# Routed attention and a gelu layer: ten sums of the first batch go to VectorE, and three batches make their first layer's combinations in PSUM

## Chip, core and metric

The kernel runs on one core of a Trainium2 chip. Its time is the device time of one execution in microseconds (us). TensorE (PE in the profile) multiplies matrices and writes to PSUM, VectorE (DVE), ScalarE (ACT) and GpSimd (POOL) work on tiles, and SyncE (SP) issues the transfers. GpSimd takes no part in PSUM work in this kernel.

## The reference, cut to what matters

```python
# q, k, v: (4 batches, 8 heads, 768, 64); centroids: (8, 16, 64)
q_assign = argmax(normalised(q) @ normalised(centroids).T)
k_assign = argmax(normalised(k) @ normalised(centroids).T)
scores = where(q_assign == k_assign, q @ k.T / 8, -1e9)
attn   = softmax(scores) @ v                       # per head
x = attn, heads side by side                       # (3072, 512)
h = x @ w_in                                       # (3072, 2048)
g = h / (1 + exp(-1.702 * h))                      # gelu, quick form
out = g @ w_out                                    # (3072, 512), float32
```

## The kernel before, in words

**Order.** Instructions are written out by hand in the order in which each engine runs them; engines wait for one another through semaphores. First comes attention for all four batches (0 to about 342 us). Its result stays in SBUF for batch 1 and is kept in DRAM (`kept`) for the others. Then come, for each batch `b` of 0 to 3, a first layer (`w_in`) and a second layer (`w_out`). This text counts batches from 1, so `b == 0` is batch 1.

**First layer.** Both layers use a block method that makes seven products of half-size blocks in place of eight (Strassen's method in the form of Winograd). For each of the eight blocks `f`, `first7` (line 848) makes seven products of two 128x384 matmuls (`product`, L854), each into a PSUM bank of its own out of the six of `ps_b`. Operands are blocks of `w_in`, sums of such blocks (`W`, made two blocks ahead on GpSimd by `sums_w`), tiles `x`, and sums of those (`Tx2`, `Tx3`, `Tx4`, also called T2 to T4; `x_steps` makes them for the next batch on VectorE during `k` = 5 and 6 of the second layer). The seven products are combined to four results, `G[:, f]` and `G[:, f + 8]` with two halves each: one ScalarE copy (L864) and seven VectorE adds with one operand in PSUM (`add`, L845), then four gelus in place (`finish`, L859). `after7(f - 1)` then makes one difference of `G` and, from `f` = 5 on, slices of the sums that the second layer needs first (`Y`, `E`).

**Second layer.** `second49(k, ...)` runs for `k` = 0 to 6, in the order `ORDER = (1, 2, 3, 6, 5, 7, 4)` of the outer products `i`. Each makes seven products of four 128x192 matmuls (L904). Three of its banks, called x, z and v, are used: after x has been copied out by ScalarE, further products are added onto what stands in it (`start=False`). The weights are blocks of `w_out`, sums of those (`Z`), and for three of the seven products sums of sums, `Wz` (three of 128x512 per `k`), which are made in batch 1 by `keep_w` on GpSimd, kept in DRAM as `kept_w`, and loaded again for each later batch by `load_sums`. For `k` = 5 and 6 of batch 1, `load_sums(k, made=True)` makes them in the tile that is used at once. During `k`, VectorE makes the four sums t3, t2, t1, t4 for `k + 1` (`sums_t`), in the steps of `extra`. At the end of `k`, the result `y` is added to the output sums `Y`:

```python
pool = nc.vector if last and i in (5, 7) else nc.gpsimd
sums(pool, {1: (),
            2: ((Y[11], y, "+", Y[22]),),
            3: ((Y[12], y, "+", Y[22]),),
            6: ((Y[12], y, "+", Y[12]), (Y[21], y, "+", Y[22])),
            5: ((Y[12], y, "+", Y[12]), (Y[22], y, "+", Y[21])),
            7: ((Y[22], y, "+", Y[22]), (Y[21], y, "+", Y[21]))}[i])
```

`last` is true in the last batch only. All elementwise sums outside PSUM go through `sums` and so have one line, L598, on whichever engine runs them; they are told apart by tile and shape. The SP queue carries all loads and stores, in the order of the program.

Of the kernel before, what the change touches and what calls it, by code (L numbers as in the profile page):

```python
# [8 lines left out]
FP32 = mybir.dt.float32  # L9
# [4 lines left out]
AF = mybir.ActivationFunctionType  # L14
# [24 lines left out]
def fast(  # L39
# [26 lines left out]
    nc = tc.nc  # L66

    B, H, S, D = q.shape
    NC = centroids.shape[1]
    DM, DF = moe_w_in.shape  # L70
    P = 128
    NJ = S // P
    HALF = S // 2
# [14 lines left out]
    FB = NF // 2  # L88
# [507 lines left out]
    def sums(engine, todo):  # L596
        for o, a, op, b in todo:
            engine.tensor_tensor(out=o, in0=a, in1=b, op=(  # L598
                ALU.add if op == "+" else ALU.subtract))
# [3 lines left out]
    def A_in(row, col, f):  # L603

        at = (row * FB + f) * P
        return w_in[:, 2 * col:2 * col + 2, at:at + P]

    w_of = {}
# [162 lines left out]
        a = W_of(i)  # L771
        sums(nc.vector, ((a(0, 1), a(0, 0), "-", a(0, 1)),))

    def keep_w(k, o):

        a = W_of(ORDER[k])
        s2, s1, s4 = o
        for i, (o, x, op, z) in enumerate((
                (s2, a(1, 1), "-", a(0, 1)), (s1, s2, "+", a(0, 0)),
                (s4, a(1, 0), "-", s2))):  # L780
            sums(nc.gpsimd, ((o, x, op, z),))
            nc.sync.dma_start(out=kept_w[k, i], in_=o)

    def spare_y():
# [5 lines left out]
    def load_sums(k, made=False):  # L790
        W[k] = ws.tile([P, 3, FQ, P], FP32, name="Wz")
        if made:
            keep_w(k, [W[k][:, i] for i in range(3)])
            return
        for i in range(3):
            nc.sync.dma_start(out=W[k][:, i], in_=kept_w[k, i])
# [47 lines left out]
    def add(o, p, a):  # L844
        nc.vector.tensor_tensor(out=o, in0=p, in1=a, op=ALU.add)  # L845

    def first7(b, f, X, T):

        S = w_of.pop(b * FB + f)

        def product(a, x):
            ps = ps_b.tile([P, 512], FP32, name="b")
            for c in range(2):
                nc.tensor.matmul(out=ps[:, 0:HALF], lhsT=a[:, c], rhs=x(c),  # L854
                                 start=(c == 0), stop=(c == 1))
            return ps[:, 0:HALF]

        def finish(g):
            nc.scalar.activation(out=g, in_=g, func=AF.Gelu_apprx_sigmoid,  # L859
                                 scale=2.0)  # L860

        g1, g2 = G[:, f], G[:, f + FB]
        p = product(A_in(0, 0, f), lambda c: X[0, 0, c])
        nc.scalar.copy(g1[:, 0], p)  # L864
        p = product(S[2], lambda c: T[2, c])
        add(g2[:, 1], p, g1[:, 0])
        p = product(S[1], lambda c: T[1, c])
        add(g1[:, 1], p, g2[:, 1])
        p = product(S[3], lambda c: T[3, c])
        add(g2[:, 0], p, g2[:, 1])  # L870
        add(g2[:, 1], p, g1[:, 1])
        p = product(S[4], lambda c: X[1, 1, c])
        add(g1[:, 1], p, g1[:, 1])
        finish(g2[:, 1])
        p = product(A_in(1, 1, f), lambda c: T[4, c])
        add(g2[:, 0], p, g2[:, 0])
        finish(g1[:, 1])
        p = product(A_in(0, 1, f), lambda c: X[1, 0, c])
        add(g1[:, 0], p, g1[:, 0])
        finish(g2[:, 0])  # L880
        finish(g1[:, 0])

    def after7(f):

# [5 lines left out]
    def second49(k, extra, last):  # L890

        i = ORDER[k]
        a, g, t, w = W_of(i), G_of(i), temps(k), W.pop(k)
        A = {1: a(0, 0), 2: a(1, 0), 3: w[:, 2], 4: a(1, 1), 5: w[:, 1],
             6: w[:, 0], 7: a(0, 1)}
        M = {1: g(0, 0), 2: g(1, 0), 3: g(1, 1), 4: t[4], 5: t[1], 6: t[2],
             7: t[3]}

        def bank_b():
            return ps_b.tile([P, 512], FP32, name="b")[:, 0:QT]  # L900

        def product(ps, n, start):
            for f in range(FQ):
                nc.tensor.matmul(out=ps, lhsT=A[n][:, f], rhs=M[n][:, f],  # L904
                                 start=start and f == 0,
                                 stop=(f == FQ - 1), skip_group_check=True)

        y = Y[22] if i == 1 else ep.tile([P, 2, HALF], FP32, name="y")
        y11, y12, y21, y22 = (y[:, m, q * QT:(q + 1) * QT]
                              for m in range(2) for q in range(2))  # L910
        p5 = ep.tile([P, QT], FP32, name="p5")
        x = bank_b()
        product(x, 1, True)
        nc.scalar.copy(y11, x)
        z = bank_b()
        product(z, 2, True)
        add(y11, z, y11)
        extra(0)
        product(x, 6, False)
        nc.scalar.copy(y12, x)  # L920
        v = bank_b()
        product(v, 5, True)
        nc.scalar.copy(p5, v)
        product(x, 7, False)
        nc.scalar.copy(y22, x)
        add(y22, y22, p5)
        extra(1)
        product(v, 3, False)
        add(y12, v, y12)
        if i == 4:  # L930
            c = Y[21]
            add(c[:, 0], y[:, 0], c[:, 0])
            add(c[:, 1, QT:], y22, c[:, 1, QT:])
            extra(2)
        product(x, 4, False)
        if i == 4:
            add(c[:, 1, 0:QT], x, c[:, 1, 0:QT])
            return
        nc.scalar.copy(y21, x)
        extra(2)  # L940
# [7 lines that stand above are left out]
# [79 lines left out]
    pend = iter(())  # L1027
    for b in range(B):
        for f in range(FB):
            first7(b, f, *XT)  # L1030
            sums_w(b * FB + f + 2)
            if f:
                after7(f - 1)
            do(pend, 1)
            if b == 0 and f < 3:
                for n in range(3 * f, min(3 * f + 3, FB)):
                    sums_z((nc.gpsimd, nc.vector, nc.vector)[n % 3], n)
            if b == 0 and f in (3, 4):
                for i in ORDER[0:4] if f == 3 else ORDER[4:]:
                    turn_w(i)  # L1040
            if b == 0 and f >= 3:
                for k in {3: (0,), 4: (1, 2), 5: (3,), 6: (4,), 7: ()}[f]:
                    keep_w(k, spare_y())
                if 5 <= f < 7:
                    load_sums(f - 5)
        after7(FB - 1)
        if b < B - 1:
            for h in range(2):
                for hp in range(HP):
                    x = xT_of[b + 1, h, hp] = xp.tile([P, HALF], FP32,  # L1050
                                                      name="x")
                    nc.sync.dma_start(out=x, in_=kept[b, h, hp])
            made = sums_x(b + 1)
        else:
            made = iter(())

        def stores(b, *todo, **how):
            for n in todo:
                store(b, n, **how)
                yield  # L1060

        def tail():
            store(b, 22)
            yield

        def chain(*todo):
            for steps in todo:
                yield from steps

        def sums_of_x():  # L1070
            for XT[:] in made:
                yield

        x_steps = sums_of_x()
        final = b == B - 1

        for k in range(7):
            nxt = sums_t(k + 1) if k < 6 else iter(())
            more = {1: sums_G(6), 2: sums_G(5), 3: sums_G(4),
                    4: stores(b, 11), 5: stores(b, 12) if final else x_steps,  # L1080
                    6: tail() if final else x_steps}.get(k, iter(()))
            if b == B - 1 and k < 2:
                test(k)
            if (b, k) == (B - 1, 6):
                is_bad = nc.values_load(bad[0:1, 0:1], min_val=0, max_val=1)

            def extra(at):
                do(nxt, (2, 1, 1)[at])
                do(more, ((1, 0, 1) if final else (0, 4, 4))[at] if k == 6
                   else (0, 0, 4)[at] if k == 2 else (0, 2, 2)[at])  # L1090

            second49(k, extra, final)
            if k < 5:
                load_sums(k + 2, b == 0 and k > 2)
            elif b < B - 1:
                load_sums(k - 5)
        pend = () if final else stores(b, 12, 22, 21)
        if final:
            store_last(b)
# [439 lines left out]
```

## Time and profile before

| what | value |
|---|---|
| median of 3 runs | 901.17 us (900.03 to 901.57) |
| profiled execution | 900.34 us |
| its span, first to last instruction | 898.5 us |
| PE, DVE, ACT, POOL busy | 885.8, 728.3, 366.1, 497.4 us |
| mean granted clock of TensorE | 0.999 |
| L845 adds on `G` (one operand in PSUM) | 224, mean 556 ns |
| L864 copies of `G` out of PSUM | 32, mean 478 ns |
| L859 gelus | 128, mean 523 ns |
| L598 POOL `Y` sums, 128x768 | 28, mean 2421 ns |

A line of a group or of an order of time names line, engine, operation, what is written and read, shape and number; a bracket gives the idle time before it and what ended it. Matmuls and weight loads are listed apart (PE, PEld), and each float32 matmul appears as two records, so a product of two matmuls has four records. Ends of matmuls are modelled; starts are the better guide. The layers of the four batches lie at about 342 to 414 and 414 to 481, 481 to 555 and 555 to 619, 619 to 691 and 691 to 755, 755 to 827 and 827 to 892 us.

### The profile page before, as it was taken

To read this page: it belongs to the slowest core of one execution; us is meant where nothing else is said; L and a number is where in the kernel's file an instruction comes from. 1 tells how busy PE (TensorE), PEld (TensorE's weight loads), DVE (VectorE), ACT (ScalarE), POOL (GpSimd) and SP (SyncE) were. 2 spreads that over 40 slices of the span, in tenths; PEclk is the share of its full clock that TensorE was granted. 3 is DMA by queue.
4 is the path that set the end of the run, shared out by engine and by line. 5 is a ranking of instruction groups with operands and counts; after the bars stand their busy time and mean duration, and the time that the engine had idled before them with its cause. 6 is when DMAs were issued, how large, how long until landed. Compare 5 with 4: busy or idle time off the path is not lost.

```text
span 898.5 us, 17781 instructions
## 1 busy us (share of the span) xinstructions
PE 885.8 (99%) x6720; PEld 581.4 (65%) x6720; DVE 728.3 (81%) x1183; ACT 366.1 (41%) x819; POOL 497.4 (55%) x469
## 2 busy tenths in 40 slices
PE   8999999999999999999999999999999999999997
PEld 3444444444444445558996557998556998556996
DVE  4999989999999997998998556798556798556795
ACT  3677767777677764322111232111232111222111
POOL 5899999998999998693274221143121134120130
PEclk9999999999999999999999999999999999999999
DMA  9566556666575310036113202223202223200224
GB/s 175 122 129 112 103 120 130 143 143 133 133 139 119 85 43 19 0 122 230 71 54 107 52 1 71 84 74 107 53 1 70 73 76 117 43 10 0 71 71 109
DMA packets 176333, 78.97 MB, mean 88 GB/s; under 512 B 152824, under 2 KB 159472, under 8 KB 176240
## 3 DMA queue, kind: packets, MB, share of 16 engines
q1 hardware_dynamic: 175984, 77.63, 35.2%
q8 instruction: 55, 0.90, 0.4%
q14 instruction: 38, 0.31, 0.1%
q10 hardware_dynamic: 256, 0.13, 0.1%
HBM read 61.03 MB, written 16.70 MB: 87 GB/s over the span
## 4 chain that ended last, share of the span: by engine, by line
PE 87%; DVE 8%; issue 2%; POOL 1%; DMA 1%; ACT 0%; SPq 0%; DVEq 0%; ACTq 0%; POOLq 0%
PE b L854 32%; PE b L904 23%; PE s L472 13%; PE o L537 12%; PE s L495 3%; PE m L554 3%; DVE G L598 2%; DVE E L598 2%; POOL sum L521 1%; PE m L348 1%; DVE Tx L598 1%; DMA in<-in_k_dram 1%; DVE x L598 0%; DVE e L200 0%; DVE y L845 0%
## 5 line engine op out<-in xcount | busy, mean ns | idle before, releaser
L521 POOL TENSOR_TENSOR sum<-sum,A 128x384 f32<-128x384 f32 x252 | 265.5, 1091 | 25.7 <-ACT A L503 16.6
L845 DVE TENSOR_TENSOR G<-b,G 128x384 f32<-128x384 f32 x224 | 123.1, 556 | 98.7 <-PE b L854 89.5
L503 ACT ACTIVATE A<-s 128x768 f32<-128x768 f32 x192 | 146.3, 809 | 91.1 <-PE s L495 71.0
L598 POOL TENSOR_TENSOR Y<-y,Y 128x768 f32<-128x768 f32 x28 | 67.4, 2421 | 175.0 <-DVE y L845 151.0
L859 ACT ACTIVATE G<-G 128x384 f32<-128x384 f32 x128 | 66.3, 523 | 199.1 <-DVE G L845 197.7
L472 PE MATMUL s<-T,T 64*64 64x384 f32 x1536 | 142.9, 487 | 0.7 <-ACT A L503 0.7
L537 PE MATMUL o<-A,inv 64*64 64x384 f32 x1536 | 141.2, 483 | 0.0
L598 POOL TENSOR_TENSOR W<-w_in 128x256 f32<-128x256 f32 x32 | 23.6, 737 | 163.8 <-PE b L854 163.5
L598 DVE TENSOR_TENSOR G<-G 128x768 f32<-128x768 f32 (+1 forms) x92 | 104.5, 1159 | 0.0
L472 PEld LDWEIGHTS s<-T,T 64*64 64x64 f32 x1536 | 54.9, 132 | 70.1 <-ACT A L503 36.4
L854 PE MATMUL b<-x,W 128*128 128x384 f32 x256 | 93.1, 486 | 0.0
L854 PE MATMUL b<-Tx,w_in 128*128 128x384 f32 x256 | 93.1, 486 | 0.0
L854 PE MATMUL b<-x,w_in 128*128 128x384 f32 x256 | 88.6, 486 | 0.0
L537 PEld LDWEIGHTS o<-A,inv 64*64 64x64 f32 x1536 | 58.3, 133 | 38.5 <-issue 33.5
L854 PEld LDWEIGHTS b<-x,W 128*128 128x128 f32 x256 | 48.6, 190 | 33.9
L854 PEld LDWEIGHTS b<-Tx,w_in 128*128 128x128 f32 x256 | 48.6, 190 | 33.9
L854 PEld LDWEIGHTS b<-x,w_in 128*128 128x128 f32 x256 | 48.5, 190 | 33.5 <-issue 0.6
L904 PE MATMUL b<-G,w_out 128*128 128x192 f32 x320 | 55.9, 326 | 0.0
L904 PEld LDWEIGHTS b<-G,w_out 128*128 128x128 f32 x320 | 52.7, 190 | 1.1
L904 PE MATMUL b<-E,Wz 128*128 128x192 f32 x288 | 51.5, 328 | 1.4 <-DVE E L598 1.4
L904 PEld LDWEIGHTS b<-E,Wz 128*128 128x128 f32 x288 | 47.1, 190 | 3.4 <-POOL Wz L598 1.3
L854 PE MATMUL b<-Tx,W 128*128 128x384 f32 x128 | 46.6, 487 | 1.5 <-DVE Tx L598 1.5
(169 smaller groups left out, 1366.4 us busy)
## 6 DMA issues: line engine op xcount, KB each, us to landing
Wz<-kept_w SPq DMA_DIRECT2D x78, 256.0 KB
raw<-in_moe_w_in_dram SPq DMA_DIRECT2D x16, 512.0 KB
raw<-in_moe_w_out_dram SPq DMA_DIRECT2D x16, 512.0 KB
inv<-in_v_dram SPq DMA_DIRECT2D x16, 384.0 KB
in<-in_q_dram SPq DMA_DIRECT2D x60, 96.0 KB
in<-in_k_dram SPq DMA_DIRECT2D x60, 96.0 KB
kept<-x SPq DMA_DIRECT2D x24, 192.0 KB
x<-kept SPq DMA_DIRECT2D x24, 192.0 KB
```

The source lines that it names most:

```text
L348: nc.tensor.matmul(out=ps[r:r + SQ, w * NJ * SQ:(w + 1) * NJ * SQ] .rearrange("p (j t) -> p j t", t=SQ), lhsT=cT[:, p % HP].rearrange("p a ...
L472: nc.tensor.matmul(out=ps[c:c + D, a, 0:HALF], lhsT=T[p, 1][rows, kt * P + c:kt * P + c + D], rhs=T[p, 0][rows, h * HALF:(h + 1) * HALF], ...
L495: nc.tensor.matmul(out=s_of[u][c:c + D, a, :], lhsT=rows_of[1, p % 2][rows, kt * P + c:kt * P + c + D], rhs=rows_of[0, p % 2][rows, h * HA ...
L503: nc.scalar.activation(out=A_of[u], in_=s_of.pop(u), func=AF.Exp, scale=SCALE)
L521: nc.gpsimd.tensor_tensor(out=sum_of[g][:, a], in0=(A_of[u - 1] if kt == 1 else sum_of[g])[:, a], in1=A_of[u][:, a], op=ALU.add)
L537: nc.tensor.matmul(out=o_of[g][a * D:(a + 1) * D, r, 0:HALF], lhsT=v_in[p][rows, a, kt, :], rhs=A[rows, a, :], start=(kt == 0), stop=(kt = ...
L554: nc.tensor.matmul(out=ps[a * D:(a + 1) * D, 0:HALF], lhsT=twos, rhs=sm[:, a, :], start=(i == 0), stop=(i == len(parts) - 1))
L598: engine.tensor_tensor(out=o, in0=a, in1=b, op=(ALU.add if op == "+" else ALU.subtract))
L845: nc.vector.tensor_tensor(out=o, in0=p, in1=a, op=ALU.add)
L854: nc.tensor.matmul(out=ps[:, 0:HALF], lhsT=a[:, c], rhs=x(c), start=(c == 0), stop=(c == 1))
L859: nc.scalar.activation(out=g, in_=g, func=AF.Gelu_apprx_sigmoid, scale=2.0)
L904: nc.tensor.matmul(out=ps, lhsT=A[n][:, f], rhs=M[n][:, f], start=start and f == 0, stop=(f == FQ - 1), skip_group_check=True)
```

## The change

Three edits. In `load_sums`, the sums `Wz` that batch 1 makes for its own `k` = 5 and 6 are made by VectorE instead of GpSimd (six instructions). In batch 1, as in the last batch already, VectorE instead of GpSimd adds `y` to the output sums for `i` = 5 and 7 (four instructions). And batches 2 to 4 use a new `first7_psum`: the same seven products, in another order, into three banks x, z and v, where x takes four products one upon another and v two; the results are read between them. It has three ScalarE copies and three VectorE adds in place of one and seven, and one of the four gelus reads PSUM. Batch 1 keeps `first7`.

```diff
-    def keep_w(k, o):
+    def keep_w(k, o, engine=nc.gpsimd):
...
-            sums(nc.gpsimd, ((o, x, op, z),))
+            sums(engine, ((o, x, op, z),))
             nc.sync.dma_start(out=kept_w[k, i], in_=o)
...
         if made:
-            keep_w(k, [W[k][:, i] for i in range(3)])
+            keep_w(k, [W[k][:, i] for i in range(3)], nc.vector)
             return
...
+    def first7_psum(b, f, X, T):
+
+        S = w_of.pop(b * FB + f)
+
+        def product(ps, a, x, start=True):
+            for c in range(2):
+                nc.tensor.matmul(out=ps, lhsT=a[:, c], rhs=x(c),
+                                 start=start and c == 0, stop=(c == 1),
+                                 skip_group_check=True)
+
+        def bank_b():
+            return ps_b.tile([P, 512], FP32, name="b")[:, 0:HALF]
+
+        def finish(g, ps=None):
+            nc.scalar.activation(out=g, in_=g if ps is None else ps,
+                                 func=AF.Gelu_apprx_sigmoid, scale=2.0)
+
+        g1, g2 = G[:, f], G[:, f + FB]
+        x, z, v = (bank_b() for _ in range(3))
+        product(x, A_in(0, 0, f), lambda c: X[0, 0, c])
+        nc.scalar.copy(g1[:, 0], x)
+        product(z, A_in(0, 1, f), lambda c: X[1, 0, c])
+        add(g1[:, 0], z, g1[:, 0])
+        product(x, S[2], lambda c: T[2, c], False)
+        nc.scalar.copy(g1[:, 1], x)
+        finish(g1[:, 0])
+        product(v, S[1], lambda c: T[1, c])
+        nc.scalar.copy(g2[:, 1], v)
+        product(x, S[3], lambda c: T[3, c], False)
+        add(g2[:, 1], x, g2[:, 1])
+        finish(g2[:, 1])
+        product(v, S[4], lambda c: X[1, 1, c], False)
+        add(g1[:, 1], v, g1[:, 1])
+        finish(g1[:, 1])
+        product(x, A_in(1, 1, f), lambda c: T[4, c], False)
+        finish(g2[:, 0], x)
...
-            first7(b, f, *XT)
+            (first7_psum if b else first7)(b, f, *XT)
...
-            second49(k, extra, final)
+            second49(k, extra, b in (0, B - 1))
```

## The prediction, made before the result

> **What bounds the kernel now.** I first read the page's busy shares and its chain of waits, then the stage table (busy time per stretch), then the order of time on each engine in the stages that the change touches.
>
> ```profile
> PE 885.8 (99%) x6720; PEld 581.4 (65%) x6720; DVE 728.3 (81%) x1183; ACT 366.1 (41%) x819; POOL 497.4 (55%) x469
> PE 87%; DVE 8%; issue 2%; POOL 1%; DMA 1%; ACT 0%; SPq 0%; DVEq 0%; ACTq 0%; POOLq 0%
> ```
>
> TensorE (PE) is busy 99%; VectorE (DVE) holds 8% of the chain. The stage table (stretch, length, busy time of PE, weight loads, DVE, ACT and POOL with their records, granted clock, DMA) says where: batch 1's second layer (413 to 484) is not full of PE, batch 2's two layers are.
>
> ```profile
> 413.00:484.00 71.00, 68.06 (x402) 65.19 (x401) 65.16 (x79) 13.30 (x39) 31.33 (x16) 1.00 0.34 116
> 484.00:555.00 71.00, 71.00 (x223) 41.93 (x222) 41.16 (x83) 19.56 (x38) 17.16 (x24) 1.00 0.14 34
> 555.00:619.00 64.00, 64.00 (x393) 63.58 (x393) 58.28 (x77) 11.37 (x35) 19.16 (x8) 1.00 0.29 89
> ```
>
> So first layers of batches 2 to 4 have nothing to win: VectorE is busy 41 of 71 us there, wholly beside TensorE. What can be won lies in PE's holes around 462 to 484 (order of time, PE; start, length, idle before):
>
> ```profile
> 462.87 1.54 PE L904 MATMUL b<-Tx,Wz 128*128 128x192 f32 x8
> 465.08 1.54 PE L904 MATMUL b<-E,Wz 128*128 128x192 f32 x8 [0.67 <-DVE E L598]
> 473.15 1.57 PE L904 MATMUL b<-E,Wz 128*128 128x192 f32 x8
> 475.40 1.54 PE L904 MATMUL b<-E,Wz 128*128 128x192 f32 x8 [0.68 <-DVE E L598]
> 480.68 1.45 PE L854 MATMUL b<-x,w_in 128*128 128x384 f32 x4
> 483.62 1.56 PE L854 MATMUL b<-Tx,W 128*128 128x384 f32 x4 [1.49 <-DVE Tx L598]
> ```
>
> A second-layer product (8 records) lasts 1.30 us start to start, a first-layer product (4 records) 1.29. Late starts therefore: 0.11 at 462.87, 0.91 at 465.08, 0.20 at 473.15, 0.95 at 475.40, and 0.07 twice in the products behind: 2.31. At 483.62 (due 481.97): 1.65. Together 3.96 us. Check: this second layer runs 414.33 to 480.68, 66.35 us; batch 2's 554.67 to 618.63, 63.96; the difference of 2.39 is the 2.31 plus 0.08 at its start.
>
> All of it waits for VectorE, and VectorE is late because GpSimd (POOL) runs:
>
> ```profile
> 461.87 1.98 POOL L598 TENSOR_TENSOR Wz<-w_out,Wz 128x512 f32<-128x512 f32 x1
> 477.68 4.47 POOL L598 TENSOR_TENSOR Y<-y,Y 128x768 f32<-128x768 f32 x2 [1.30 <-DVE y L845]
> 460.81 1.91 DVE L598 TENSOR_TENSOR Tx<-G 128x768 f32<-128x768 f32 x1
> 600.28 0.96 DVE L598 TENSOR_TENSOR Tx<-G 128x768 f32<-128x768 f32 x1
> 478.32 4.24 DVE L598 TENSOR_TENSOR x<-x 128x384 f32<-128x384 f32 x2
> ```
>
> The sum at 460.81 takes 1.91 us beside GpSimd's `Wz`; the same sum of batch 2, without it, 0.96.
>
> **What the Trainium skill says.** "SBUF — State Buffer", Who interferes with whom: VectorE with two SBUF inputs and a GpSimd instruction that reads SBUF exclude each other for a whole instruction. The trace agrees: 4.24 us for two `x` sums beside 4.47 us of GpSimd; adds with a PSUM operand keep 0.34. "PSUM — Partial Sum Buffer", The four PSUM rules: a synchronised read in the middle of an accumulation group is allowed; `second49` already does it, without holes in batches 2 to 4. "TensorE: Matmul & The Clock Gate", Step-by-step: weights are loaded ahead of the running matmul; here 0.32 us ahead (501.46 for 501.78).
>
> **Part one: sums moved from GpSimd to VectorE (batch 1, k=3 to 5).** Moved: six `Wz` sums (128x512) and four `Y` sums (128x768); k=3's two `Y` sums (453.17 to 458.0) stay on GpSimd. Price on VectorE: `Y` 0.95 each, 0.87 apart (the last batch runs them so: two in 1.81 at 883.92). `Wz`: the skill's "VectorE: DVE Perf Modes", TRN2 errata, gives (N+151)/0.96 ns, 691 for 512; two of that size took 1.28 at 379.35. Estimate per three: 0.70 (the second needs the first) + 0.62 + 0.60 = 1.92. Added: 2x1.92 + 4x0.88 = 7.4 us. Freed, taking from each slow row the time that the same row has with GpSimd idle: beside `Wz`, G 0.8, Tx 0.95, y 1.07, then y 1.07, E 1.08, Tx 1.08; beside the `Y` sums, G and E (2.30 and 2.45, 0.95 alone) 2.85, and the two `x` (4.24, 1.01 alone) 3.23: 12.1 us. Net, VectorE gains 4.7 us. If each `Wz` sum took that page's full 0.691, 0.3 us of it would go, no more.
>
> Replay from 458.76, where k=3's slow `G` sums end: `Wz` to 460.68, y 460.95, t3 461.93, t2 (`Tx`) ends 462.88, t1 (`E`) 464.02. PE's product due at 462.76 starts about 463.03 (0.27 late), the next, due 464.33, finds t1 in time. Transposes, y, t4 to 466.0; `Y` to 467.8; `Wz` to 469.7; y, t3, t2 ends 471.89 against a product due at 472.13: its load is 0.05 late. t1 473.02, due 473.48; then `Tx`, y, t4, `x`, `Y` to 477.7; y, y 478.2; T2 479.2. PE ends the layer at 478.68. `first7_psum` puts A(0,1) second, so T2 is wanted at 481.26 instead of 479.97: no wait. Left: 0.32 of 3.96. **Gain 3.65.** The stores of `kept_w` on SP now wait for VectorE, at 460 to 470 instead of 460 to 476; behind them on SP stand the first `Wz` loads of batch 2, used after 540; behind the moved sums on POOL stood only `sums_w` of batch 2, which waits for PE until 489.13 anyway. Bounds for part one: 3.96 if nothing is late, and 1.65 if T2 is in time but the waits inside the second layer all stay.
>
> **Part two: `first7_psum`, 24 blocks.** Per block 4 adds of 0.556 go, 53 us of VectorE in all; 2 ACT copies of 0.48 come, 23 us of ScalarE. A gelu that reads PSUM is not in the trace; it lies between the 0.48 of such a copy and the 0.52 of the gelu from SBUF, or a little outside, and ScalarE waits anyway. TensorE: the same 14 matmuls, 9.03 us a block. Both engines have room, so the value is zero by itself; the question is the new waits, since bank x is now refilled after each read. Times from a block's start (a consumer starts 0.20 after a product's slot ends, as 501.98 and 500.69 show):
>
> ```profile
> 499.20 2.74 PE L854 MATMUL b<-x,w_in 128*128 128x384 f32 x8
> 500.69 0.56 DVE L845 TENSOR_TENSOR G<-b,G 128x384 f32<-128x384 f32 x1 [0.73 <-PE b L854]
> 501.98 0.48 ACT L864 COPY G<-b 128x384 f32<-128x384 f32 x1 [0.17 <-PE b L854]
> ```
>
> First copy of x 1.49 to 1.97, refill at 2.58. Second copy 4.07 to 4.55, refill 5.16. Copy of v 5.36 to 5.84 (the gelu before it ends 5.1), refill 6.45. VectorE's add from x 6.65 to 7.21, refill 7.74. A refill must be released 0.32 ahead, and 0.11 passes from VectorE's end to the load (464.94, 465.05): the margins are 0.18, 0.18, 0.18 and 0.10, with 0.13 more before the load (0.19 long) shows. Behind a waiting refill stands all of TensorE. I take zero; bounds: 0 and 0.2 x 24 = 4.8 us. A gain in steady state is excluded, PE having no hole there.
>
> At the end of each of these layers PE now waits 0.26 for the last `E` slice (the `E,Wz` group at 557.27 lasts 3.02 instead of 2.76). With four adds fewer, the slice can be ready 1.2 earlier, but in batches 2 and 3 GpSimd's `sums_w`, now starting at 8.0 of the block instead of 6.7, falls beside `after7` and stretches it by about 1.0 (three rows of 0.35 to 0.55 become 0.8 to 1.1, as at 397 to 400). Estimate: 0.14 + 0.14 + 0.26 = 0.5 gained; bounds minus 1.0 to plus 0.8, all of the present waits.
>
> Sum: 3.65 + 0.5 = 4.15. The profiled execution, 900.34 (span 898.5), would become 896.2; it lies 0.83 under the median of the three runs, 901.17 (900.03 to 901.57), so 897.0.
>
> **Rivals.**
> - **Partial loss.** The refills are late by 0.09 to 0.25 us a block: 2.2 to 6 us eat the gain; 899 to 903. For: margins of 0.1 to 0.2. Against: `second49` re-accumulates the same way with 0.32 copies and shows no hole. At 0.12, 900.0.
> - **Slower: the refill after VectorE's add.** It has the thinnest margin, and VectorE's `after7`, now beside `sums_w`, could still be running. At 0.5 us in each of 24 blocks: 12 - 4.15 = +7.9, 909. It decides from 4.15/24 = 0.17 us a block. Against: `after7` should end by 11.5 at the latest, 2.5 into the next block, and the add comes at 6.65.
> - **VectorE is too full.** If the slow rows are not the lock's doing, moving adds 7.4 us to VectorE before T2: 1.65 + 7.4 - 1.29 = 7.8 late instead of 1.65, +6, 907. Against: the same rows are short in batch 2 wherever GpSimd is idle.
>
> **Chances.** Main case 0.76 (895.6 to 898.7), partial loss 0.11, slower refill 0.09, full VectorE 0.04. A measurement tells 0.2%, 1.8 us, from no change. Faster takes the main case and a sliver of the partial one: 0.77; same 0.10; slower 0.13. The range 895.5 to 901.0 takes in the main case and half of the partial one.
>
> **What would show it.** Right: batch 1's second layer about 64.3 us long instead of 66.35, no wait for `Tx` at the first block of batch 2, no GpSimd work after 458 in that layer, first layers of 72.2 us, VectorE's busy time down some 57 us. Wrong: idle PE before the third, fifth, sixth or seventh product of the blocks, put down to ACT's copy or VectorE's add; or `E,Wz` groups of that layer waiting as before.

## The result, and the profile after

The kernel takes 895.72 us after the change (median of six runs, 894.57 to 896.72) against 900.12 before (six runs, 899.32 to 901.57). The ratio is 0.9950, with a 95% interval of 0.9939 to 0.9961: 3.5 to 5.5 us less, 4.40 by the medians. Forecast were 4.15 less, and 897.0 as the time.

The profiled execution took 895.92 us (span 894.1). Its busy times and chain, the same two lines as were shown of the kernel before:

```profile
PE 883.0 (99%) x6720; PEld 581.9 (65%) x6720; DVE 678.4 (76%) x1097; ACT 385.6 (43%) x867; POOL 482.0 (54%) x459
PE 94%; DVE 4%; issue 1%; DMA 1%; ACT 0%; SPq 0%; ACTq 0%; DVEq 0%
```

TensorE's share of the chain rises from 87% to 94%, VectorE's falls from 8% to 4%. In order of time, the chain of the kernel before runs through VectorE, with short pieces of issue, from 430.81 to 483.57; in the kernel after it leaves VectorE for good at 462.70, just ahead of the one product in that stage that is still clearly late. The share itself is no price: 4% of the span is 36 us, and the time fell by 4.4, because TensorE was busy beside nearly all of that stretch. The stage table of the kernel after (columns as before: stretch, length, busy of PE, weight loads, DVE, ACT, POOL, clock, DMA share and GB/s):

```profile
413.00:484.00 71.00, 70.80 (x414) 67.46 (x414) 63.00 (x95) 14.34 (x42) 10.88 (x6) 1.00 0.34 116
484.00:555.00 71.00, 71.00 (x234) 43.46 (x233) 28.47 (x54) 26.07 (x55) 18.84 (x24) 1.00 0.15 39
```

In the first stretch PE's busy time was 68.06 and is 70.80 of 71: the holes are all but gone. In the second, PE stays full, VectorE falls from 41 to 28 us and ScalarE rises from 20 to 26: the second edit's exchange, which buys nothing by itself in a stretch where PE was full already. The order of time of PE in the kernel after shows the places of the old holes (start, length, idle before):

```profile
462.84 1.54 PE L941 MATMUL b<-Tx,Wz 128*128 128x192 f32 x8
464.21 1.46 PE L941 MATMUL b<-E,Wz 128*128 128x192 f32 x8
...
472.01 2.76 PE L941 MATMUL b<-E,Wz 128*128 128x192 f32 x16
...
478.51 2.74 PE L889 MATMUL b<-x,w_in 128*128 128x384 f32 x8
481.09 1.45 PE L889 MATMUL b<-Tx,W 128*128 128x384 f32 x4
```

No line has a bracket. One product lasts 1.30, and the two ahead of the group at 462.84 start at 459.94, so it was due at 462.54 and is 0.30 late; the group behind it starts 1.37 after it instead of 1.30, another 0.07. All later products stand 1.30 apart (the two `E,Wz` products at 472.01 last 2.60). T2's product starts at 481.09, which is exactly 478.51 plus two products of 1.29.

VectorE's order of time in the same stretch (kernel after) shows why:

```profile
459.88 0.69 DVE L598 TENSOR_TENSOR Wz<-w_out,Wz 128x512 f32<-128x512 f32 x1
...
461.73 0.96 DVE L598 TENSOR_TENSOR Tx<-G 128x768 f32<-128x768 f32 x1
...
474.80 1.02 DVE L598 TENSOR_TENSOR x<-x 128x384 f32<-128x384 f32 x2
475.74 1.82 DVE L598 TENSOR_TENSOR Y<-y,Y 128x768 f32<-128x768 f32 x2
```

The `Tx` sum that took 1.91 beside GpSimd takes 0.96, and the two `x` sums take 1.02 instead of 4.24. The work that was added is short: 0.69 for a `Wz` sum, 1.82 for two `Y` sums.

**A measure without the start.** In the profiled executions attention ends anywhere from 340.0 to 342.2 us, in code that is the same up to there. So the spans are compared from the first `b<-x,w_in` matmul of batch 1 to the first matmul of the last transposes ("layers' time" below): 341.98 to 891.14 before, 549.16 us; 341.76 to 886.60 after, 544.84. The difference, 4.32, agrees with the 4.40 of the medians. Of it, 1.95 is batch 1's second layer (66.35 to 64.40), 1.75 is the wait for T2 with the product behind it (1.65 and 0.10), and 0.62 lies in the last slices of `E` (below).

### The profile page after: what moved, and what is told of

Read it like the earlier page. It is cut to its first block, busy times and chain, and to the rows that moved or that the text cites. A ratio compares the mean times of both kernels' runs of the same rounds, so it can differ in the third digit from the quotient of the medians.

```text
span 894.1 us, 17678 instructions
## 1 busy us (share of the span) xinstructions
PE 883.0 (99%) x6720; PEld 581.9 (65%) x6720; DVE 678.4 (76%) x1097; ACT 385.6 (43%) x867; POOL 482.0 (54%) x459
## 4 chain that ended last, share of the span: by engine, by line
PE 94%; DVE 4%; issue 1%; DMA 1%; ACT 0%; SPq 0%; ACTq 0%; DVEq 0%
PE b L941 25%; PE b L889 24%; PE s L472 14%; PE o L537 14%; PE b L854 8%; PE s L495 3%; PE m L554 3%; DVE G L598 2%; PE m L348 1%; DVE E L598 1%; DMA in<-in_k_dram 1%; DVE Tx L598 0%; PE o L296 0%; DVE G L845 0%; DVE y L845 0%
## 5 line engine op out<-in xcount | busy, mean ns | idle before, releaser
L521 POOL TENSOR_TENSOR sum<-sum,A 128x384 f32<-128x384 f32 x252 | 266.0, 1092 | 24.9 <-ACT A L503 16.4
L845 DVE TENSOR_TENSOR G<-b,G 128x384 f32<-128x384 f32 x128 | 69.5, 556 | 142.0 <-PE b L889 135.7
L598 POOL TENSOR_TENSOR Y<-y,Y 128x768 f32<-128x768 f32 x24 | 58.1, 2435 | 165.8 <-DVE y L845 141.9
L889 PE MATMUL b<-x,W 128*128 128x384 f32 x192 | 69.8, 486 | 0.0
L889 PE MATMUL b<-Tx,w_in 128*128 128x384 f32 x192 | 69.8, 486 | 0.0
L889 PE MATMUL b<-x,w_in 128*128 128x384 f32 x192 | 65.8, 486 | 0.0
L897 ACT ACTIVATE G<-G 128x384 f32<-128x384 f32 x72 | 37.7, 524 | 52.1 <-DVE G L845 52.1
L941 PE MATMUL b<-G,w_out 128*128 128x192 f32 x320 | 55.9, 326 | 0.0
L941 PEld LDWEIGHTS b<-G,w_out 128*128 128x128 f32 x320 | 52.7, 190 | 1.1
L889 PEld LDWEIGHTS b<-x,W 128*128 128x128 f32 x192 | 36.5, 190 | 25.4
L889 PEld LDWEIGHTS b<-Tx,w_in 128*128 128x128 f32 x192 | 36.5, 190 | 25.4
L889 PEld LDWEIGHTS b<-x,w_in 128*128 128x128 f32 x192 | 36.4, 190 | 24.6
L941 PE MATMUL b<-E,Wz 128*128 128x192 f32 x288 | 50.5, 327 | 0.1
L941 PEld LDWEIGHTS b<-E,Wz 128*128 128x128 f32 x288 | 47.3, 190 | 0.6 <-DVE E L598 0.4
L495 PE MATMUL s<-rows,rows 64*64 64x384 bf16 x720 | 45.6, 323 | 0.0
```

The lines of the kernel that those rows point to most:

```text
L495: nc.tensor.matmul(out=s_of[u][c:c + D, a, :], lhsT=rows_of[1, p % 2][rows, kt * P + c:kt * P + c + D], rhs=rows_of[0, p % 2][rows, h * HA ...
L521: nc.gpsimd.tensor_tensor(out=sum_of[g][:, a], in0=(A_of[u - 1] if kt == 1 else sum_of[g])[:, a], in1=A_of[u][:, a], op=ALU.add)
L598: engine.tensor_tensor(out=o, in0=a, in1=b, op=(ALU.add if op == "+" else ALU.subtract))
L889: nc.tensor.matmul(out=ps, lhsT=a[:, c], rhs=x(c), start=start and c == 0, stop=(c == 1), skip_group_check=True)
L897: nc.scalar.activation(out=g, in_=g if ps is None else ps, func=AF.Gelu_apprx_sigmoid, scale=2.0)
L941: nc.tensor.matmul(out=ps, lhsT=A[n][:, f], rhs=M[n][:, f], start=start and f == 0, stop=(f == FQ - 1), skip_group_check=True)
```

## Experiments

Diffs are against the changed kernel. Behind an added line the line numbers are one higher (L846 for L845, L942 for L941). "Before" in a ratio is the kernel before on the same chip.

### Which edit brings it: e1_sums_only and e2_psum_only

e1 keeps the sums on VectorE and takes the old `first7` for all batches; e2 keeps `first7_psum` and gives the ten sums back to GpSimd.

```diff
e1  -            (first7_psum if b else first7)(b, f, *XT)
    +            first7(b, f, *XT)
e2  -            keep_w(k, [W[k][:, i] for i in range(3)], nc.vector)
    +            keep_w(k, [W[k][:, i] for i in range(3)])
    -            second49(k, extra, b in (0, B - 1))
    +            second49(k, extra, final)
```

> Part one alone: ten sums of batch 1 on VectorE, first7 in all four batches. My theory (GpSimd's sums held VectorE up; 3.6 us of the 4.2 us seen in the traces come from this part): batch 1's second layer 64.4 us, T2 ready about 478.9 and wanted at 479.8, so no hole at the first block of batch 2; the 0.26 us holes at the E slices stay. About 3.6 us faster than before. Rival (the new first layer is what brings it, since it wants T2 later): a hole of about 1 us stays before T2 and the gain is 2.0 us or less.

> Part two alone: first7_psum in batches 2 to 4, the ten sums stay on GpSimd. My theory: batch 1's second layer keeps its 66.3 us; T2 is ready at 483.6 as before but wanted one product later, at 483.26, so 0.4 us of the 1.65 us hole is left; the E slices gain 0.6. About 1.8 us faster than before. Rival (53 us less VectorE work is worth something in itself): more than 3 us faster.

Measured: e1 895.93 us, ratio 0.9961 (0.9947 to 0.9975), layers' time 545.45, 3.71 less than before. e2 898.36, ratio 0.9983 (0.9975 to 0.9990), layers' time 547.63, 1.53 less. PE's order of time, e1 first, then e2:

```profile
477.66 1.45 PE L854 MATMUL b<-x,w_in 128*128 128x384 f32 x4
478.95 1.45 PE L854 MATMUL b<-Tx,W 128*128 128x384 f32 x4
```

```profile
463.12 1.54 PE L941 MATMUL b<-E,Wz 128*128 128x192 f32 x8 [0.67 <-DVE E L598]
...
473.44 1.54 PE L941 MATMUL b<-E,Wz 128*128 128x192 f32 x8 [0.69 <-DVE E L598]
...
478.71 2.74 PE L889 MATMUL b<-x,w_in 128*128 128x384 f32 x8
481.75 1.53 PE L889 MATMUL b<-Tx,W 128*128 128x384 f32 x4 [0.29 <-DVE Tx L598]
```

In e1, T2 is wanted one product earlier than in the changed kernel and is still in time: 478.95 is 477.66 plus 1.29. In e2 the two waits for `E` are those of the kernel before, and of the wait for T2 0.46 is left (481.75 against 478.71 + 2.58): the later place of T2 alone hides 1.19 of the 1.65. The two edits overlap there, so their gains, 3.71 and 1.53, don't add to 4.32 but to 5.24. The sums on VectorE bring nearly all of it; of the second edit only the earlier `E` slices remain, 4.32 - 3.71 = 0.6. (In e2 itself, 1.53 - 1.19 = 0.34; a hole at 485.92, which the changed kernel hasn't, takes about the rest, 0.23 and 0.10 in the product behind it. There a late VectorE add, at 484.39, holds up a gelu, and the gelu the copy that frees bank v, at 485.40: the chain that e9 below shows at length.)

### Are both kinds of sum needed: e3_wz_only and e4_y_only

Both take the old `first7`. e3 moves only the six `Wz` sums to VectorE, e4 only the four `Y` sums.

```diff
e3  -            second49(k, extra, b in (0, B - 1))
    +            second49(k, extra, final)
e4  -            keep_w(k, [W[k][:, i] for i in range(3)], nc.vector)
    +            keep_w(k, [W[k][:, i] for i in range(3)])
```

> Only the six Wz sums move to VectorE; the Y sums stay on GpSimd, first7 in all batches. By replay with the lock: the holes at the first E group of k=5 shrink to 0.3, but GpSimd's Y sums (i=5) now hold the Wz sums up, so k=6 gets a hole of about 1.6, and T2 one of about 1.0: about 1.0 us faster than before. If instead every moved sum only adds its own time to VectorE, slower than before by about 2 us.

> Only the four Y sums move to VectorE; the Wz sums stay on GpSimd, first7 in all batches. By replay: GpSimd makes the second Wz set right behind the first, from 463.9 on, beside t1 of k=5, so the hole there grows to about 1.9; from then on VectorE is free of GpSimd and T2 is in time. About 2.0 us faster than before. If instead every moved sum only adds its own time to VectorE, slower by about 2 us.

Measured: e3 897.39, ratio 0.9975 (0.9967 to 0.9983), layers' time 1.97 under before. e4 898.02, ratio 0.9978 (0.9970 to 0.9985), 1.92 under. e4 is as expected; e3 gained twice what was expected. First e3's PE and DVE order of time, then e4's PE:

```profile
471.76 2.84 PE L941 MATMUL b<-E,Wz 128*128 128x192 f32 x16 [1.02 <-DVE E L598]
```

```profile
464.37 2.30 DVE L598 TENSOR_TENSOR Wz<-w_out 128x512 f32<-128x512 f32 x1
```

```profile
465.80 1.54 PE L941 MATMUL b<-E,Wz 128*128 128x192 f32 x8 [1.74 <-DVE E L598]
```

In e3 the `Wz` sum that VectorE now makes stands beside GpSimd's `Y` sums and takes 2.30 instead of 0.68: a sum that is moved is cheap only where nothing of GpSimd's runs beside it. PE is then 1.18 late at 471.76 (due 470.58), and T2 is 0.42 late, beside the 0.30 that the changed kernel has too. e4 has one wait of size, 1.98 late at 465.80, and none for T2. Half of the gain each, 3.89 together against e1's 3.71: the two moves are close to additive here. e3's expectation put the two remaining waits at 1.6 and 1.0; they were 1.18 and 0.42.

### Is it GpSimd that makes the rows slow: e5_pool_reads and e6_pool_writes

The rival was that VectorE was simply too full. If so, work on GpSimd should not matter. So the changed kernel, with all its sums where they are, gets work on GpSimd that nothing waits for: 17 sums that read `w_in` (e5), or 34 memsets of the same tile (e6), from the end of `k` = 3.

```diff
+    dead = sp.tile([P, HALF], FP32, name="dead")
...
             second49(k, extra, b in (0, B - 1))
+            if b == 0 and k == 3:
e5 +                for _ in range(17):
+                    sums(nc.gpsimd, ((dead, w_in[:, 0, 0:HALF], "+", w_in[:, 1, 0:HALF]),))
e6 +                for _ in range(34):
+                    nc.gpsimd.memset(dead, 0.0)
```

> The changed kernel, and after k=3 of batch 1 GpSimd makes 17 sums of 128x384 of two slices of w_in into a tile that nobody reads. If the lock between GpSimd's reads and VectorE's two-input sums is the cause: VectorE's two-input rows between 458 and T2 grow by about 1.1 us each as long as the 17 last, T2 comes 10 to 18 us late, and the kernel takes 905 to 912, slower than before although VectorE has the same work as in the changed kernel. Rival (the gain came from the order or from GpSimd's late results, not from port use): no change, 895.7.

> The changed kernel, and after k=3 of batch 1 GpSimd fills the same dead tile 34 times with zeros: it writes SBUF and reads nothing. If only GpSimd's reads exclude VectorE's second input, no row of VectorE is slower and the time is that of the changed kernel, 895.7. If any GpSimd use of SBUF holds VectorE up, VectorE's rows grow and the time goes above 900.

Measured: e5 908.63, ratio 1.0100 (1.0079 to 1.0121), layers' time 556.15, 11.3 over the changed kernel. e6 896.03, ratio 0.9953 (0.9934 to 0.9972), layers' time 544.76, the changed kernel's within 0.1. The orders of time of POOL, DVE and PE in e5:

```profile
456.60 25.63 POOL L598 TENSOR_TENSOR dead<-w_in 128x384 f32<-128x384 f32 x17
```

```profile
461.59 0.35 DVE L846 TENSOR_TENSOR y<-b,y 128x192 f32<-128x192 f32 x1
...
463.37 1.63 DVE L598 TENSOR_TENSOR Tx<-G 128x768 f32<-128x768 f32 x1
464.92 1.15 DVE L846 TENSOR_TENSOR y<-y,p 128x192 f32<-128x192 f32 x1
```

```profile
465.14 2.05 PE L942 MATMUL b<-Tx,Wz 128*128 128x192 f32 x8 [3.62 <-DVE Tx L598]
```

and of POOL and DVE in e6:

```profile
458.09 16.14 POOL L1133 MEMSET dead<- 128x384 f32 x34
```

```profile
462.06 0.96 DVE L598 TENSOR_TENSOR Tx<-G 128x768 f32<-128x768 f32 x1
```

VectorE does the same work in all three kernels. Beside GpSimd's reads the `Tx` sum takes 1.63 and the small sum of two SBUF tiles (`y<-y,p`) 1.15 instead of 0.35; beside GpSimd's writes they keep 0.96 and 0.35, though GpSimd is as busy. The add that has one operand in PSUM (`y<-b,y`) keeps its 0.35 beside the reads too. PE then waits 3.62 for `Tx` and, at 481.52, 3.19 for `E`. The "too full" rival falls: the waits, some 8 us with the shorter ones, are made by work that VectorE has no part in. It is the neighbour that counts, and of the two kinds tried only the one that reads SBUF.

Not all of the 11.3 us are such waits. TensorE's granted clock, 1.00 in this stage of the changed kernel, is 0.67, 0.50 and 0.69 in the stretches 465 to 468, 468 to 471 and 471 to 474 of e5, just behind the wait of 3.62. Three products in a row there take 2.65, 2.72 and 2.46 from start to start where 1.30 is due. With the 0.60 of waiting that lies among them taken off, the low clock cost about 3.3 us. All four runs of e5 have a lower mean clock than the rest, 0.991 to 0.995 for 0.996 and more.

### How much room has the refill of bank x: e7_delay_64 and e8_delay_384

The prediction held VectorE's add out of bank x to be the thinnest margin of `first7_psum`, 0.10 plus 0.13. An extra VectorE copy of 64 or 384 columns stands ahead of it in each of the 24 blocks.

```diff
+        nc.vector.tensor_copy(out=z[:, 0:64], in_=x[:, 0:64])      # e8: 384
         add(g2[:, 1], x, g2[:, 1])
```

> The changed kernel with one more VectorE instruction in each block of first7_psum, between the fifth product and the add that reads x: a copy of 64 columns of x into bank z, whose values are not used again. It delays the release of bank x by about 0.1 to 0.15 us. The prediction's margin there was 0.10, with 0.13 more before a late weight load shows: no hole, 895.7 to 896.2. If the refill was already at its limit, 24 x 0.1 = 2.4 us or more slower than the changed kernel.

> As the run with 64 columns, with 384: the add comes about 0.46 us later. Past the margin of 0.23 by 0.23 us in each of 24 blocks: about 5.5 us slower than the changed kernel, 901. If the margin is larger than thought, less; if an add on its way to a refill can't hold TensorE up, 895.7.

Measured: e7 895.35, ratio 0.9949 (0.9930 to 0.9969), layers' time 544.80, no loss. e8 897.69, ratio 0.9972 (0.9965 to 0.9980), layers' time 546.82, 1.98 over the changed kernel. A block lasts 9.12 us in e8 for 9.03, so it loses 0.09 where 0.23 were expected (24 of these are 2.2 us; 0.16 comes back, as the `E` groups of batches 2 and 3 are no longer 0.08 late). The add in the changed kernel, then in e8:

```profile
548.44 0.56 DVE L845 TENSOR_TENSOR G<-b,G 128x384 f32<-128x384 f32 x1 [3.31 <-PE b L889]
```

```profile
549.03 0.55 DVE L845 TENSOR_TENSOR G<-b,G 128x384 f32<-128x384 f32 x1
```

The order of time of the weight loads in e8, and its list of waits (us in total, times, longest):

```profile
549.63 0.94 PEld L889 LDWEIGHTS b<-Tx,w_in 128*128 128x128 f32 x4 [0.44 <-DVE G L845]
```

```profile
PEld b L889 <- DVE G L845: 10.6, 24, 0.4
```

The wait is there in all 24 blocks, and it is the one that the rival named; it is the size of the margin that was wrong. The delay is counted from the product that the add reads: it starts at 546.88 in the changed kernel and at 547.07 in e8, so the add ends 2.12 and 2.51 after it. That is 0.39 later and not the copy's whole 0.48, since the copy begins 0.08 sooner behind the product than the add alone does. (In e7 the add ends 2.18 after its product, only 0.06 later.) If what is past the room costs its full length, the room is 0.39 - 0.09 = 0.30, not 0.23. Three terms moved. The add comes 0.07 later than the prediction had it (1.56 behind the start of its product for 1.49). The load starts 0.05 after VectorE's end (549.58 to 549.63), where 0.11 had been taken from another place. And in e8 the load is listed only 0.01 ahead of the matmul, which starts as due at 549.64 and lasts 1.54 for 1.45. A load that runs 0.10 ahead would then cost nothing, where 0.19, its own length, had been taken: 0.23 - 0.07 + 0.06 + 0.09 = 0.31. This last term is an estimate from e8; no run delays the add by something between 0.06 and 0.39.

### Where three banks do cost: e9_all_psum

The change leaves batch 1 with `first7`. e9 gives it `first7_psum` too.

```diff
-            (first7_psum if b else first7)(b, f, *XT)
+            first7_psum(b, f, *XT)
```

> The changed kernel with first7_psum in batch 1 too. VectorE has 3.8 to 5.6 us of other sums after each of batch 1's blocks (sums_z, turn_w, after7 slowed by GpSimd), all in line ahead of the next block's add from z. By replay that add comes at 4 to 5.5 us of the block instead of 2.78; where it is past about 5.1, gelu and the copy of v behind it are late and the sixth product waits: 0.1 to 0.6 us in four or five blocks, 2 us in all, against 0.34 won at the E slice: 1 to 2 us slower than the changed kernel, 897 to 898. Rival (the fewer adds help where VectorE is fullest): 0.3 us faster than the changed kernel.

Measured: 904.10, ratio 1.0051 (1.0038 to 1.0064), slower than the kernel before; layers' time 552.36, 7.5 over the changed kernel. The direction was expected, the size was several times that. Batch 1's first layer lasts 80.07 us (342.10 to 422.17) where the other batches' lasts 72.24. PE's order of time:

```profile
348.01 1.53 PE L889 MATMUL b<-Tx,W 128*128 128x384 f32 x4 [3.06 <-ACT G L903]
...
362.68 1.53 PE L889 MATMUL b<-x,W 128*128 128x384 f32 x4 [1.01 <-ACT G L910]
...
373.43 1.53 PE L889 MATMUL b<-x,W 128*128 128x384 f32 x4 [1.48 <-ACT G L910]
...
392.43 1.53 PE L889 MATMUL b<-x,W 128*128 128x384 f32 x4 [0.70 <-ACT G L910]
```

Against the due starts these are 3.33, 1.18, 1.65 and 0.87 late; with 0.45 at 352.40 they make 7.5. How one of them comes about is read from DVE and ACT in e9:

```profile
371.82 0.54 DVE L845 TENSOR_TENSOR G<-b,G 128x384 f32<-128x384 f32 x1
```

```profile
372.39 0.52 ACT L897 ACTIVATE G<-G 128x384 f32<-128x384 f32 x1 [2.51 <-DVE G L845]
372.82 0.46 ACT L910 COPY G<-b 128x384 f32<-128x384 f32 x1
```

In batch 1 VectorE also makes sums of `w_out`. The add from z stands behind them and comes at 371.82; the gelu (L897) waits for it; ScalarE's copy of v (L910) stands behind that gelu in ScalarE's queue, though its own product is long done; and the refill of v at 373.43 waits for the copy. The 3.33 of the first block was not foreseen: ScalarE's first copy comes at 347.39, which the profile puts down to GpSimd's `W` sums. The kernel before has the same late copy (347.29), but there the next products go into other banks, and PE runs on without a hole. The 0.45 at 352.40 has a cause of its own: a table load of 1.28 us on ScalarE (350.07) stands ahead of the first gelu, and the copy of v behind it comes at 351.79. In this stage six banks absorb a late reader; three that are refilled within the block do not.

### A version a little further: e10_i6_too

Most of what is left in the middle of the changed kernel's batch 1, 0.30 and 0.07 at 462.84, comes from `k` = 3's `Y` sums (`i` = 6), which stay on GpSimd. (A hole of 0.33 at 419.64, at the last `E` slice of batch 1's first layer, is in both kernels.) The edit acts in batches 1 and 4.

```diff
-        pool = nc.vector if last and i in (5, 7) else nc.gpsimd
+        pool = nc.vector if last and i in (5, 6, 7) else nc.gpsimd
```

> The changed kernel with the two Y sums of i=6 (k=3) on VectorE too, in batches 1 and 4. In batch 1 they hold two G sums up (5.04 us for two, 1.82 alone) just ahead of the Wz sums. On VectorE they take 1.77: VectorE is 1.4 us earlier, and the hole of 0.30 plus 0.07 us at the Tx group of k=5 goes. 0.3 to 0.4 us faster than the changed kernel: 895.3; the difference is at the edge of what the runs tell, the trace should show it. Rival: in batch 4 the same edit delays something that was in time, and the sum is 0 or a loss.

Measured: 895.24, ratio 0.9955 (0.9941 to 0.9968), layers' time 544.44, 0.40 under the changed kernel. PE and DVE in e10:

```profile
460.75 1.47 PE L941 MATMUL b<-G,w_out 128*128 128x192 f32 x8
462.05 1.47 PE L941 MATMUL b<-Tx,Wz 128*128 128x192 f32 x8
```

```profile
453.10 1.82 DVE L598 TENSOR_TENSOR G<-G 128x768 f32<-128x768 f32 x2
454.83 1.82 DVE L598 TENSOR_TENSOR Y<-y,Y 128x768 f32<-128x768 f32 x2
```

The group starts 1.30 after the one before, as due; the two `G` sums, 5.04 in the changed kernel (453.59), take 1.82. Batch 4 shows no new wait. The trace shows the 0.4 us; the times of whole executions can't tell it from the changed kernel.

## Why the prediction was right, point by point

- **What bounds it.** Right: TensorE, with its holes around batch 1's second layer, at the start of batch 2 and at the `E` slices. e1 alone has 3.71 of the 4.32 us.
- **Part one, 3.65.** Measured 3.70: 1.95 in the second layer, 1.65 at T2 and 0.10 in the product behind T2's (485.01 in the kernel before), a term that the sum of 3.96 had left out. The replay held well; this layer starts 0.22 earlier in the profiled execution after (414.11 for 414.33), and with that taken off, the layer's end at 478.68 is 478.46, 478.51 measured, and T2 at 479.2 is 478.98, 479.03 measured (478.01 and 1.02 for the two `Tx` sums). Left over were 0.30 for the 0.27 at the `Tx` group and another 0.07 behind it; the 0.05 foreseen in `k` = 6 didn't come. Three `Wz` sums took 1.92 (458.56 to 460.48), as estimated. VectorE's busy time from the layer's first product to the end of the `Tx` sums went from 64.84 to 60.08 us, 4.8 less, for the 4.7 of the prediction. The cause, GpSimd's reads beside VectorE's two-input sums, is shown by e5 and e6.
- **"All of it waits for VectorE."** Not quite. The 0.20 at 473.15 waits for GpSimd's own result: its first `Wz` sum of `k` = 6 runs from 471.12 to 473.10, while VectorE's `E` for that product is done at 471.96. In the kernel before, on GpSimd and on VectorE:

```profile
471.12 1.98 POOL L598 TENSOR_TENSOR Wz<-w_out 128x512 f32<-128x512 f32 x1
```

```profile
469.51 2.45 DVE L598 TENSOR_TENSOR E<-G 128x768 f32<-128x768 f32 x1
```

The weight load of that product starts at 473.15, after 0.33 of waiting that the profile puts down to this `Wz`. So moving the sums cured two things, slow neighbours and one late result. How much later GpSimd's result would have been than needed with VectorE's rows fast, no run shows.
- **"T2 in time" had two grounds, and one is enough.** e1 has T2 in time without the new order of products, so that the change puts A(0,1) second did not matter once the sums had moved.
- **Part two, zero in steady state.** Right: the first layers take 72.24 us, 9.03 a block, without a hole; the gelu that reads PSUM takes 0.49 (L897), inside the 0.48 to 0.52 taken. The margin behind that zero was mis-sized: 0.23 in the text, about 0.30 by e8. The partial-loss and slower-refill rivals did not come true, but e8 shows that their mechanism is real once the add ends 0.39 us later.
- **The end of the first layers, 0.5.** Measured 0.62: PE's group at that place in batches 2 to 4 lasted 3.02, and after the change 2.85, 2.84 and 2.76. The line of batch 2, from PE's order of time in the kernel after:

```profile
553.35 2.85 PE L941 MATMUL b<-E,Wz 128*128 128x192 f32 x16
```

- **VectorE's busy time, minus 57.** It fell by 50. The count of adds is right (224 to 128 at 556 ns, 53.6 us less), and so is part one's 4.8. The step that failed: `after7` beside `sums_w` was priced only at the end of the layer. It now stretches in more blocks: from the groups of both kernels, the 32 differences `G<-G` of 128x384 went from 19.1 to 22.3 us, and of the slices of 128x192, `Y<-G` from 7.2 to 10.9 and `E<-Y,G` from 7.1 to 9.9, 9.7 us more in all. In a stage that PE bounds this cost no time.
- **The absolute time.** 897.0 was forecast from the median of three runs, 901.17. The median of six was 900.12, so 1.05 of the 1.28 us between 897.0 and 895.72 is the starting point; the gain differs by the other 0.2 (4.15 against 4.40 by the medians, 4.32 by the traces).

## What to carry to other kernels

Price a sum that is moved between VectorE and GpSimd by what it does to the rows beside it, not by its own length: here VectorE's busy time in batch 1's second layer and up to T2's and T4's sums fell by 4.8 us although some 7.5 us of sums were added to it. Before cutting the operations of an engine, look at whether that engine ends a wait in that stage: the second edit took 53 us off VectorE and brought 0.6. And when banks are refilled within a block, count every reader between the fill and the refill, with what stands ahead of each in its queue; where other work of uneven length shares those queues, as in batch 1, more banks were worth their copies.

## What was not expected of the hardware

- **The exclusion isn't of whole instructions.** In e5 GpSimd's 17 sums take 25.63 us. Two of them take 0.99, as do the shortest of GpSimd's sums in attention (L521), so alone the 17 would need some 17 us. VectorE's sums of two SBUF tiles that ran within that time come to about 12.3 us at their lengths in the changed kernel (six `Wz` 4.1, two `G` 1.9, one `Tx` 1.0, three `E` 2.9, two `Y` 1.8, two `y<-y,p` 0.7). 17 + 12.3 = 29.3 doesn't fit into 25.63 if only one may run at a time, so by this estimate nearly 4 us ran side by side; shared over 33 instructions, 0.11 each. "SBUF — State Buffer" in the Trainium skill says that a two-input VectorE sum contends with a GpSimd instruction that reads but not with one that only writes (Who interferes with whom), and that whichever of the two starts first has the shared ports for the whole instruction (SBUF: two separate sides). The first is what e5 and e6 show. For the second, the measurement decides: "for a whole instruction", as the prediction has it too, is too strong for the lengths that the profile lists. A long sum grew by 0.5 to 0.8, not by the whole 1.0 of its neighbour.
- **A refill of PSUM needs less notice than the load's lead suggests.** Loads run 0.32 ahead of their matmul, yet loads that are listed only 0.01 ahead (e8, 549.63 for 549.64) cost 0.09 us a block.
- **A long wait of TensorE can cost more than itself.** Behind the wait of 3.62 us in e5 the granted clock of the next three stretches of 3 us was 0.67, 0.50 and 0.69 (about 3.3 us lost); behind the waits of 3.19 in e5 (481.52) and 3.06 in e9 (348.01) it was 1.00. What decides it, these runs don't show.
